# Column halves for scores and weight grams, transposes in transpose mode, and a new order of the first steps, in an attention and feed-forward kernel on one core

## The chip, the cores and the metric

The program runs on one core of a Trainium2 chip. The time is device time in microseconds (us) of one execution, and the number given for a kernel is a median over runs: for the kernel before 741.81 us, of three runs from 740.6 to 742.11. TensorE, VectorE, ScalarE, GpSimd and SyncE are called PE, DVE, ACT, POOL and SP, as the profile does; PEld is the load of the stationary operand of a matmul.

## The reference

The inputs are float32: q, k, v (4 batches, 8 heads, 768 positions, 64 per head), 8 memory keys and values, and the weights of two mixing layers. Each chunk of 32 queries sees 8 memory keys and 56 neighbours, 64 keys in all.

```python
for c in range(768 // 32):
    l, r = max(0, 32 * c - 16), min(768, 32 * c + 32 + 8)
    scores = scale * q[:, :, 32 * c:32 * c + 32] @ concat(mem_k, k[:, :, l:r]).T
    a = softmax(scores)
    out[:, :, 32 * c:32 * c + 32] = a @ concat(mem_v, v[:, :, l:r])
x = out with its heads side by side                      # 4 x 768 x 512
gate = sigmoid(causal convolution of x over 5 steps, per channel)
x = (gate * (x @ w_val)) @ w_out                         # 512 x 512 each
xn = (x - mean) / sqrt(var + 1e-6) * g_ln
out = x + relu(xn @ w_ch1) @ w_ch2                       # 512 x 2048, 2048 x 512
```

The four weight matrices and the convolution come as words of 8 bytes, which the kernel turns into float32 itself.

## The kernel before

The 3072 positions are cut into 24 sub-blocks of 128 (`SUB`), which are grouped into 13 blocks: the first of one sub-block, eleven of two, the last of one. Each block goes through three streams. Attention (`a`): scores into PSUM (`s_ps`), maximum, difference and Exp into `sc`, `normalize`, a transpose to `pT`, and the product with v (`pv`), which ACT and DVE copy to `xT`. Mixing (`x`, in `mix`): the gate `gt` as a chain of five taps on ACT and DVE, `val` = x times `Wv`, the output product `yps`, its statistics and the normalised `xn`. Feed-forward (`f`): `ch1` writes `c_ps`, ACT and DVE make `h` of it, and `ch2` adds into `acc`.

Matmuls come in two kinds. The first sub-blocks use float32 operands: the attention of the first five (`attention32`, as `NA32` counts three blocks), the mixing of the first two blocks, the feed-forward of block 0. All others use a pair of float16 tiles, a high and a low part, in three passes (`PASSES`), so that a score of one head pair and group takes three matmuls. A score matmul has both chunks of a group as its 128 output rows (`bd`, block-diagonal, 2 chunks x 2 heads x 32 queries) and all 96 keys of the group as columns. Of these each chunk uses 64: four copies on ACT (L251) pick them out of two PSUM tiles, and DVE takes the maximum (L254) and the difference (L255) from `sc` in SBUF.

Before the float16 kind can start, each weight needs one power of two as its scale, which is found from the sum of its squares. A weight arrives in pieces of 1 MB (20 in all); each is converted by ACT (`top`, L162) and DVE (L163), and PE then sums its squares as the diagonal of a gram matrix: eight matmuls of 128 x 128 per piece (L198, tile `gram`). `weight_scale` multiplies with `eye` and reduces (L205, L206). Then `split_weight` makes the two parts (ACT L218, DVE L219). Four float32 transposes of 128 x 128 make `pT` (L331) in the first five sub-blocks, and `xnT` (L538) in the first two blocks; they are matmuls with `eye`. Later transposes go by DMA.

The order of work is written out by hand. `PLAN` is a string of steps: `w` starts the fetch of a weight piece, `l` the loads of a sub-block, `m`, `1` and `2` take a step of the mixing weights, of the first and of the second feed-forward weight, and `a`, `x`, `f` a step of the three streams. After `PLAN` the string `STEADY` is walked through once for each block. A scheduler then puts the instructions of each engine in a fixed order, and each engine runs its own list strictly in that order. `fill` issues idle matmuls at the start (`FILLS`). `ps` is a pool of four PSUM tiles for scores, transposes, `pv`, `val` and `yps`.

Of the kernel before, what the change touches and what calls it, by code (L numbers as in the profile page):

```python
# [8 lines left out]
F32 = mybir.dt.float32  # L9
# [24 lines left out]
NA32 = 3  # L34
# [5 lines left out]
PLAN = "w1 m1 a5 m1 l1 w3 x1 w2 m1 x5 a1 l1 a2 m1 w1 x1 w1 x2 a2 m1 1_1 a1 1_1 w1 a1 w2 1_1 x1 1_1 a2 1_1 a1 1_1 x1 w1 1_1 x1 1_1 x1 2_1 l1 w1 1_1 f1 x1 w1 x4 m1 2_1 x1 w2 f1 1_1 2_1 m1 f1 2_2 x1 f1 1_2 a1 2_1 a1 x1 a1 f1 2_2 m1 w1 l1 f1 a1 1_2 f1 2_1 a1 2_1 a2 2_1 x1 1_1 m1 w1 a1 2_1 a2 1_2 2_2 f1 x1 2_3"  # L40
# [14 lines left out]
def chunk_attention_moe_kernel(ctx: ExitStack, tc: tile.TileContext,  # L55
# [34 lines left out]
    eye = const.tile([P, P], F32, name="eye")  # L90
    g_one = const.tile([P, 1], F32, name="g_one")
# [97 lines left out]
    def gram(W, j):  # L189
        if j == 0:  # L190
            tag = "acc0" if W in (Wv, W1) else "acc1"
            W.acc = ps_a.tile([P, 512], F32, tag=tag, name="gram")
            W.gram = W.acc[:, 0:P]

        w = W.src(j).bitcast(BF16).rearrange("p (n w) -> p n w", w=2)
        for c in range(8):
            x = w[:, c * P:(c + 1) * P, 1]
            nc.tensor.matmul(out=W.gram, lhsT=x, rhs=x, start=(j == 0 and c == 0), stop=(j == W.n - 1 and c == 7))  # L198

    def weight_scale(W, bits, name, factor=None):  # L200
# [4 lines left out]
        nc.vector.tensor_tensor(out=diag, in0=W.gram, in1=eye, op=ALU.mult)  # L205
# [21 lines left out]
    first16 = sum(sizes[:NA32])  # L227
# [15 lines left out]

    def exponentials(i, s_ps, c_exp):
# [50 lines left out]
    def attention32(n, d, u):  # L295
# [11 lines left out]
        for e in range(2):  # L307
# [52 lines left out]
    def attention(n, d, u):  # L360
# [45 lines left out]
        s_ps = []  # L406
        for g in range(2):
            t = ps.tile([P, HP, KEYS], F32, tag="ps", name="s_ps")
            for hp in range(HP):
                for x, (r0, r1) in enumerate(PASSES):  # L410
                    nc.tensor.matmul(out=t[:, hp, :],  # L411
                                     lhsT=bd[r0][:, hp, g].rearrange("p c e q -> p (c e q)"),
                                     rhs=k2[r1][:, hp, g, :], start=(x == 0), stop=(x == 2))
            s_ps.append(t)
# [39 lines left out]
    def open_block(j):  # L454
        d = blk[j] = {"T": blocks[j][1] * SUB, "iv": {}, "split": j > 0, "f32": j < NF32, "a32": j < NA32}
# [3 lines left out]
        return d  # L459

    def mix(j):
# [5 lines left out]
        for hp in range(HP):  # L467
# [11 lines left out]
        nc.scalar.activation(out=gt[:, :, 0:T], in_=gt[:, :, 0:T], func=AF.Tanh, scale=0.5)  # L479
# [6 lines left out]
        for w in range(2):  # L486
# [17 lines left out]
        xn = d["xn"] = [xn_p.tile([P, KC, 2 * SUB], F16, tag=f"xn{r}", name=f"xn{r}") for r in range(2)] if d["split"] else \  # L504
            [b_p.tile([P, KC, 2 * SUB], F16, tag="hg0", name="xnf").rearrange("p k t -> p (k t)").bitcast(F32).rearrange("p (k t) -> p k t", t=SUB)]
        mv = sm_p.tile([P, 2, 2], F32, tag="mv", name="mv")
        for u in range(n):
# [12 lines left out]
            if u == n - 1:  # L520
# [10 lines left out]
        for u in range(n):  # L531
# [3 lines left out]
            if j < NPET:  # L535
                t = ps.tile([P, KC, P], F32, tag="ps", name="xnT")
                for kc in range(KC):
                    nc.tensor.matmul(out=t[:, kc, :], lhsT=xh[:, kc * P:(kc + 1) * P], rhs=eye, start=True, stop=True)  # L538
                if d["split"]:
# [5 lines left out]
                nc.vector.tensor_tensor(out=xn[0], in0=t, in1=g_sb.rearrange("p (k o) -> p k o", o=1).to_broadcast([P, KC, P]),  # L545
                                        op=ALU.mult)
# [13 lines left out]
    def ch1(d, w):  # L560
# [70 lines left out]
    if True:  # L631
# [17 lines left out]
        pieces = [(W, jj) for W in (Wv, Wo, W1, W2) for jj in range(W.n)]  # L649
        fetched = [0]  # L650
# [91 lines left out]
        to_f32(cw_raw, cw_sb.rearrange("p k c -> p (k c)"))  # L742
        count = dict.fromkeys(streams, 0)
# [3 lines left out]
        per = {"a": lambda j, n: (5 if j < NA32 else 8) * n, "x": lambda j, n: 8 + 2 * n, "f": lambda j, n: NM * n * SUB // 256}  # L747
# [61 lines left out]
```

## Time and profile before

| | |
|---|---|
| median of 3 runs | 741.81 us (740.6 to 742.11) |
| the profiled execution: its time | 740.43 us |
| its span | 738.6 us |
| chain that ended last, share of PE | 85% |
| the same, share of DVE, ACT | 8%, 5% |
| DMA, mean over the span | 91 GB/s |

The profiled execution took 740.43 us, of which the span, from the first to the last recorded instruction, is 738.6 us. The chain that ended last is followed back from the last instruction to whatever released it; an engine with a high share of it is the one whose work set the end. Busy time alone says less: matmuls are pipelined, so that the start of one row and the start of the next give a better duration than the row's own length, which has the pipeline's drain in it.

### The profile page before, as it was taken

What the parts mean: (1) busy time and instruction counts of PE and PEld (TensorE: products, weight loads), DVE (VectorE), ACT (ScalarE), POOL (GpSimd) and SP (SyncE); (2) the same over time, 40 slices, a digit from 0 to 9 for tenths busy, and PEclk for the clock granted to TensorE, in tenths of its full rate; (3) what the DMA queues carried; (4) which work ended last, traced back from release to release, by engine and by line L of the source; (5) the groups of instructions that cost most, each with busy time, mean ns of one, the idle gap of its engine ahead of it and who ended that gap; (6) DMA issues with size and microseconds to landing.
All of it is one profiled execution on the core that took longest, in us unless ns stands there. A gap on an engine that the chain in (4) does not pass through costs nothing.

```text
span 738.6 us, 15525 instructions
## 1 busy us (share of the span) xinstructions
PE 724.9 (98%) x6461; PEld 512.1 (69%) x6461; DVE 509.2 (69%) x1124; ACT 392.5 (53%) x684; POOL 10.6 (1%) x35
## 2 busy tenths in 40 slices
PE   8889999999999999999999999999999999999998
PEld 7777676667767757757757767767767766767676
DVE  4979989768658768768668668668667668651321
ACT  5867967647537537537546546546555554420210
POOL 2000010000000000000000000000000000000000
PEclk9999999999999999999999999999999999999999
DMA  9992623142132133132142153043043011010010
GB/s 357 417 401 109 228 65 89 37 113 72 52 79 86 37 86 94 34 89 95 29 95 94 19 104 94 16 100 101 16 101 100 16 30 43 16 29 30 1 43 15
DMA packets 62262, 67.08 MB, mean 91 GB/s; under 512 B 45680, under 2 KB 45936, under 8 KB 62192
## 3 DMA queue, kind: packets, MB, share of 16 engines
q1 hardware_dynamic: 61904, 66.07, 29.5%
q8 instruction: 50, 0.82, 0.5%
q14 instruction: 20, 0.16, 0.1%
q10 hardware_dynamic: 288, 0.02, 0.0%
HBM read 49.30 MB, written 6.29 MB: 75 GB/s over the span
## 4 chain that ended last, share of the span: by engine, by line
PE 85%; DVE 8%; ACT 5%; issue 1%; DMA 0%; ACTq 0%; DVEq 0%
PE acc L598 32%; PE c_ps L570 32%; PE yps L511 8%; PE val L493 7%; PE s_ps L411 2%; PE pv L441 2%; DVE gt L475 2%; DVE w L163 1%; ACT top L162 1%; PE pv L345 1%; ACT w L218 1%; ACT sc L251 1%; DVE w L219 1%; ACT xT L289 1%; DMA g_sb<-in_g_ln_dram 0%
## 5 line engine op out<-in xcount | busy, mean ns | idle before, releaser
L598 PE MATMUL acc<-w,h 128*128 128x512 f16 (+3 forms) x1184 | 267.0, 377 | 0.1
L570 PE MATMUL c_ps<-xn,w 128*128 128x256 f16 (+1 forms) x2304 | 254.8, 268 | 0.0
L570 PEld LDWEIGHTS <-w 128*128 128x128 f16 x2304 | 215.4, 98 | 36.9 <-issue 0.6
L598 PEld LDWEIGHTS <-h 128*128 128x128 f16 x1152 | 109.5, 98 | 114.1 <-DVE h L575 1.8
L575 DVE SCALAR_TENSOR_TENSOR h<-c_ps,h 128x512 f16<-128x512 f32 x92 | 62.9, 683 | 54.0 <-ACT h L573 53.9
L573 ACT ACTIVATE h<-c_ps 128x512 f16<-128x512 f32 (+1 forms) x96 | 56.5, 588 | 79.1 <-PE c_ps L570 77.5
L475 DVE SCALAR_TENSOR_TENSOR gt<-xT,cw_sb,gt 128x256 f32<-128x256 f32 (+1 forms) x208 | 83.4, 458 | 1.6 <-ACT gt L471 1.5
L511 PE MATMUL yps<-wo,hg 128*128 128x512 f16 x252 | 58.3, 379 | 0.2
L493 PE MATMUL val<-x,wv 128*128 128x256 f16 (+1 forms) x528 | 56.9, 268 | 0.0
L493 PEld LDWEIGHTS <-wv 128*128 128x128 f16 x528 | 49.7, 98 | 5.5
L251 ACT ACTIVATE sc<-s_ps 64x256 f32<-64x256 f32 x96 | 36.2, 377 | 25.4 <-PE s_ps L411 22.5
L511 PEld LDWEIGHTS <-hg 128*128 128x128 f16 x252 | 23.2, 98 | 26.7 <-DVE hg L499 0.6
L377 ACT ACTIVATE vs<-vt 128x1024 bf16<-128x1024 f32 x19 | 19.9, 1048 | 39.8 <-PE pv L441 39.8
L498 ACT ACTIVATE hg<-gt 128x512 f16<-128x512 f32 (+1 forms) x22 | 13.4, 610 | 47.2 <-DVE gt L495 47.2
L550 ACT ACTIVATE xh<-xh 128x512 f16<-128x512 f32 x21 | 13.2, 630 | 44.8 <-DMA xn<-xh 23.8
L605 DVE SCALAR_TENSOR_TENSOR y<-acc,co_w,y 128x512 f32<-128x512 f32 (+2 forms) x24 | 16.5, 725 | 28.9 <-PE acc L598 28.8
L551 DVE TENSOR_TENSOR xh<-xh,xh 128x512 f16<-128x512 f32 x21 | 14.5, 692 | 27.4 <-DMA xn<-xh 19.5
L291 DVE TENSOR_SCALAR xT<-pv,c_pv 64x256 f32<-64x256 f32 x38 | 17.0, 488 | 19.3 <-ACT xT L289 19.2
L422 ACT ACTIVATE p<-sc 128x512 f16<-128x512 f32 x19 | 12.0, 630 | 33.0 <-DVE sc L270 32.9
L393 DVE SCALAR_TENSOR_TENSOR bd<-qt,s,bd 64x512 f16<-64x512 f32 x38 | 28.3, 744 | 0.7
L495 DVE SCALAR_TENSOR_TENSOR gt<-gt,val 128x512 f32<-128x512 f32 (+1 forms) x26 | 16.6, 646 | 15.7 <-PE val L493 15.7
L392 ACT ACTIVATE bd<-qt,s 64x512 f16<-64x512 f32 x38 | 27.1, 712 | 0.5
(136 smaller groups left out, 809.8 us busy)
## 6 DMA issues: line engine op xcount, KB each, us to landing
vt<-in_v_dram SPq DMA_DIRECT2D x24, 512.0 KB, 3.9
kt<-in_k_dram SPq DMA_DIRECT2D x24, 384.0 KB, 3.6
qt<-in_q_dram SPq DMA_DIRECT2D x24, 256.0 KB, 2.7
out_dram<-y SPq DMA_DIRECT2D x23, 256.0 KB, 2.1
w<-in_w_ch_dram SPq DMA_DIRECT2D x5, 1023.5 KB, 9.3
raw<-in_w_ch_dram SPq DMA_DIRECT2D x4, 1023.8 KB, 13.5
w<-in_w_ch_dram SPq DMA_DIRECT2D x4, 1023.8 KB, 14.2
raw<-in_w_ch_dram SPq DMA_DIRECT2D x3, 1023.5 KB, 5.3
```

Source lines behind the costliest of these rows:

```text
L251: nc.scalar.activation(out=by_group[pp, :, g, :], in_=s_ps[g][pp, :, ch * CHUNK:ch * CHUNK + NSEEN], func=AF.Copy)
L291: nc.vector.tensor_scalar(out=o, in0=t[pp, :, :, e, :], scalar1=c_pv if isinstance(c_pv, float) else c_pv[pp], scalar2=None, op0=ALU.mult)
L377: nc.scalar.activation(out=v2[0].bitcast(BF16), in_=vt, func=AF.Square, accum_out=ss[:, 2:3])
L392: nc.scalar.activation(out=hi, in_=src, func=AF.Copy, scale=s[pp, 0:1])
L393: nc.vector.scalar_tensor_tensor(out=lo, in0=src, scalar=s[pp, 0:1], in1=hi, op0=ALU.mult, op1=ALU.subtract)
L475: nc.vector.scalar_tensor_tensor(out=o, in0=xT[:, hp, 0:n, kk:kk + SUB], scalar=cw_sb[:, kk, hp:hp + 1], in1=o, op0=ALU.mult, op1=ALU.add)
L493: nc.tensor.matmul(out=t[:, u, 0:T], lhsT=l, rhs=r, start=(x == 0), stop=(x == len(todo) - 1))
L511: nc.tensor.matmul(out=t, lhsT=l, rhs=r, start=(x == 0), stop=(x == len(todo) - 1))
L570: nc.tensor.matmul(out=t[:, u * T:(u + 1) * T], lhsT=l, rhs=r, start=(x == 0), stop=(x == len(todo) - 1))
L573: nc.scalar.activation(out=h[0], in_=t, func=AF.Relu)
L575: nc.vector.scalar_tensor_tensor(out=h[1], in0=t, scalar=0.0, in1=h[0], op0=ALU.max, op1=ALU.subtract)
L598: nc.tensor.matmul(out=a[:, 0:n], lhsT=l, rhs=r, start=(m == 0 and x == 0), stop=(m == NM - 1 and x == len(todo) - 1))
```

## The change

Scores: `scores` writes one PSUM tile of 8 x 64 columns. The two chunks of a group become two matmuls, each with 64 columns of `bd` as its stationary operand and its own 64 keys as the moving one; chunk 0 writes output partitions 0 to 63, chunk 1 partitions 64 to 127. The matmuls of a sub-block go from 24 of 128 x 96 to 48 of 64 x 64 in float16, and from 8 to 16 in float32 (each of these runs as two instructions). The four copies on ACT go; maximum and difference read PSUM.

Grams: a piece takes sixteen matmuls of 64 x 64, even column groups into partitions 0 to 63, odd into 64 to 127, and the diagonal is picked with `eye2`, two 64-wide unit matrices, which POOL makes. Transposes by PE (`flip`) use the transpose mode in place of a matmul with `eye`. The float32 `xn` of block 0 lies in two tiles of its own and is written by two instructions of half the width. `PLAN` is new, and its end now holds the steps of a block which `STEADY` held before. The branches of `QD`, `DIAG`, `POWR`, `ORDER` and `TP` are not taken; `A32` is the old `NA32`.

```diff
-NA32 = 3
+A32 = 3
+NFF = 1
+COLS = 1
+POWR = 0
+PET = 1
+GC = 1
+QD = 0
+DIAG = 0
...
-PLAN = "w1 m1 a5 m1 l1 w3 x1 w2 m1 x5 a1 l1 a2 m1 w1 x1 w1 x2 a2 m1 1_1 a1 1_1 w1 a1 w2 1_1 x1
+PLAN = "w1 a4 l1 a1 w3 m2 w1 m1 a1 x1 w1 1_1 m1 l1 x1 w1 x1 w1 x2 w1 x3 a2 w1 x1 1_1 a1 m1 a2 w1 a1
...
         w = W.src(j).bitcast(BF16).rearrange("p (n w) -> p n w", w=2)
+        if GC:
+            for c in range(16):
+                x = w[:, c * 64:(c + 1) * 64, 1]
+                o = c % 2 * 64
+                nc.tensor.matmul(out=W.gram[o:o + 64, 0:64], lhsT=x, rhs=x, start=(j == 0 and c < 2), stop=(j == W.n - 1 and c > 13))
+            return
...
+            diag = diag[:, 0:64]
+            nc.vector.tensor_tensor(out=diag, in0=W.gram[:, 0:64], in1=eye2, op=ALU.mult)
...
+    def scores(b2, k2):
+        todo = passes(range(len(b2)), range(len(b2)))
+        if COLS:
+            t = ps.tile(WIDE, F32, tag="ps", name="s_ps")
+            for hp in range(HP):
+                for g in range(2):
+                    for x, (r0, r1) in enumerate(todo):
+                        for ch in range(2):
+                            nc.tensor.matmul(out=t[ch * 64:(ch + 1) * 64, 2 * hp + g, :],
+                                             lhsT=b2[r0][:, hp, g, ch].rearrange("p e q -> p (e q)"),
+                                             rhs=k2[r1][:, hp, g, ch * CHUNK:ch * CHUNK + NSEEN],
+                                             start=(x == 0), stop=(x == len(todo) - 1))
+            return [t]
...
-        for g in range(2):
-            for ch in range(2):
-                pp = slice(ch * 64, (ch + 1) * 64)
-                nc.scalar.activation(out=by_group[pp, :, g, :],
-                                     in_=s_ps[g][pp, :, ch * CHUNK:ch * CHUNK + NSEEN], func=AF.Copy)
+        src = sc
+        if COLS:
+            src = s_ps[0]
...
-        nc.vector.tensor_reduce(out=mx, in_=sc, axis=AX.X, op=ALU.max)
-        nc.vector.tensor_tensor(out=sc, in0=sc, in1=mx.to_broadcast(WIDE), op=ALU.subtract)
+        nc.vector.tensor_reduce(out=mx, in_=src, axis=AX.X, op=ALU.max)
+        nc.vector.tensor_tensor(out=sc, in0=src, in1=mx.to_broadcast(WIDE), op=ALU.subtract)
...
+    def flip(o, x):
+        if PET:
+            nc.tensor.transpose(out=o, in_=x, identity=eye)
+        else:
+            nc.tensor.matmul(out=o, lhsT=x, rhs=eye, start=True, stop=True)
...
-            nc.tensor.matmul(out=t[:, hp, :], lhsT=sc[:, 2 * hp:2 * hp + 2, :].rearrange("p g k -> p (g k)"), rhs=eye,
-                             start=True, stop=True)
+            flip(t[:, hp, :], sc[:, 2 * hp:2 * hp + 2, :].rearrange("p g k -> p (g k)"))
...
+        if GC:
+            nc.gpsimd.tensor_tensor(out=eye2, in0=eye[:, 0:64], in1=eye[:, 64:128], op=ALU.add)
```

How the lists of the engines moved is shown at two places of DVE's list. The first is the first softmax of the kernel before; `wv` with `top` is the conversion of the first piece of that weight, whose ACT half (`top`) runs beside it:

```order
L254 TENSOR_REDUCE mx<-sc 128x8
L255 TENSOR_TENSOR sc<-sc,mx 128x512
L163 SCALAR_TENSOR_TENSOR wv<-w_113,top_115 128x1024
L259 MEMSET sc 64x4x16
L267 TENSOR_REDUCE sum<-sc 128x8
L268 TENSOR_SCALAR sum<-sum 128x8
L269 RECIPROCAL rs<-sum 128x8
L270 TENSOR_TENSOR sc<-sc,rs 128x512
```

DVE at the same place in the changed kernel, whose line numbers are its own (L304 maximum, L305 difference, L175 conversion):

```order
L304 TENSOR_REDUCE mx<-s_ps 128x8
L305 TENSOR_TENSOR sc<-s_ps,mx 128x512
L309 MEMSET sc 64x4x16
L317 TENSOR_REDUCE sum<-sc 128x8
L318 TENSOR_SCALAR sum<-sum 128x8
L175 SCALAR_TENSOR_TENSOR wv<-w_114,top_116 128x1024
L319 RECIPROCAL rs<-sum 128x8
L320 TENSOR_TENSOR sc<-sc,rs 128x512
```

The conversion has moved from ahead of the sum to behind it, ahead of the reciprocal; on ACT its `top` has moved from ahead of the Exp to behind it. The second place is DVE's list around the gate of the first block in the kernel before; the `gt<-xT` rows are the taps, the `mx` is that of the next sub-block:

```order
L475 SCALAR_TENSOR_TENSOR gt<-xT,cw_sb,gt 128x128 x13
L163 SCALAR_TENSOR_TENSOR wo<-w_113,top_115 128x1024
L475 SCALAR_TENSOR_TENSOR gt<-xT,cw_sb,gt 128x128 x2
L254 TENSOR_REDUCE mx<-sc 128x8
L475 SCALAR_TENSOR_TENSOR gt<-xT,cw_sb,gt 128x128
L255 TENSOR_TENSOR sc<-sc,mx 128x512
L163 SCALAR_TENSOR_TENSOR wo<-w_113,top_114 128x1024
L495 SCALAR_TENSOR_TENSOR gt<-gt,val 128x2x128 x2
```

DVE at the same place in the changed kernel (L561 is a tap, L582 the product with `val`):

```order
L561 SCALAR_TENSOR_TENSOR gt<-xT,cw_sb,gt 128x128 x15
L175 SCALAR_TENSOR_TENSOR wo<-w_114,top_116 128x1024
L561 SCALAR_TENSOR_TENSOR gt<-xT,cw_sb,gt 128x128
L304 TENSOR_REDUCE mx<-s_ps 128x8
L225 TENSOR_TENSOR diag<-gram,eye_102 128x64
L582 SCALAR_TENSOR_TENSOR gt<-gt,val 128x2x128 x2
L305 TENSOR_TENSOR sc<-s_ps,mx 128x512
L175 SCALAR_TENSOR_TENSOR wo<-w_114,top_116 128x1024
```

The product with `val` has moved ahead of the difference and of the second `wo` conversion, and 15 of the 16 taps, 13 before, stand ahead of the first one. SP's list, the loads and the weight pieces, stands as it did through all of this part.

## Rows read from the trace of the kernel before

**Rows 1.** The page's first part: busy us, share of the span, instructions.

```profile
PE 724.9 (98%) x6461; PEld 512.1 (69%) x6461; DVE 509.2 (69%) x1124; ACT 392.5 (53%) x684; POOL 10.6 (1%) x35
```

**Rows 2.** Busy us by stretch (from:to); clock, DMA share and GB/s last.

```profile
0.00:50.00 50.00, 40.66 (x451) 36.72 (x452) 34.85 (x85) 31.13 (x49) 4.97 (x13) 1.00 0.98 392
50.00:124.00 74.00, 72.87 (x533) 53.63 (x532) 70.20 (x131) 60.09 (x87) 2.50 (x5) 1.00 0.41 145
124.00:700.00 576.00, 575.75 (x5105) 394.85 (x5104) 395.75 (x896) 297.10 (x542) 3.17 (x17) 1.00 0.24 62
```

**Rows 3.** PE's waits: us in total, times, longest.

```profile
PE gram L198 <- DVE w L163: 2.4, 2, 2.2
PE gram L198 <- DVE wo L163: 2.2, 1, 2.2
PE s_ps L411 <- DVE ks L396: 0.5, 1, 0.5
```

**Rows 4.** Groups of PE and ACT by form: busy us, mean ns; idle before.

```profile
L411 PE MATMUL s_ps<-ks,bd 128*128 128x96 f16 x456 | 22.7, 206 | 0.5 <-DVE ks L396 0.5
...
L251 ACT ACTIVATE sc<-s_ps 64x256 f32<-64x256 f32 x96 | 36.2, 377 | 25.4 <-PE s_ps L411 22.5 <-PE s_ps L320 1.7
...
L162 ACT ACTIVATE top<-w 128x1024 f16<-128x1024 bf16 x13 | 17.5, 1356 | 1.7 <-DMA w<-in_w_val_dram 1.5
```

**Rows 5.** PE's timeline in the steady stretch: start us, us, instructions.

```profile
147.37 1.18 PE L411 MATMUL s_ps<-ks,bd 128*128 128x96 f16 x24
148.39 2.75 PE L598 MATMUL acc<-w,h 128*128 128x512 f16 x12
150.98 2.78 PE L570 MATMUL c_ps<-xn,w 128*128 128x256 f16 x24
...
158.81 5.34 PE L598 MATMUL acc<-w,h 128*128 128x512 f16 x24
164.09 0.87 PE L441 MATMUL pv<-pT,vs 64*128 64x64 f16 x48
164.89 2.79 PE L570 MATMUL c_ps<-xn,w 128*128 128x256 f16 x24
```

**Rows 6.** PE's timeline at the start: float32 forms, grams, the first float16 `c_ps`.

```profile
12.40 1.13 PE L331 MATMUL pT_ps<-eye,sc 128*128 128x128 f32 x8 [0.24 <-DVE sc L270]
...
32.81 2.00 PE L345 MATMUL pv<-pT,vt 64*128 64x64 f32 x32 [0.56 <-DVE pT L335]
34.74 2.03 PE L320 MATMUL s_ps<-kt,bd 128*128 128x96 f32 x16
36.60 0.62 PE L198 MATMUL gram<-w 128*128 128x128 bf16 x8
...
43.16 0.64 PE L198 MATMUL gram<-w 128*128 128x128 bf16 x8 [2.21 <-DVE w L163]
43.63 0.44 PE L570 MATMUL c_ps<-xnf,w 128*128 128x128 f32 x2
43.90 1.08 PE L331 MATMUL pT_ps<-eye,sc 128*128 128x128 f32 x8
44.81 1.28 PE L570 MATMUL c_ps<-xnf,w 128*128 128x128 f32 x10
...
103.48 5.08 PE L570 MATMUL c_ps<-xn,w 128*128 128x256 f16 x45
```

**Rows 7.** DVE's timeline at the first scores, and where it fills up.

```profile
7.67 0.69 DVE L254 TENSOR_REDUCE mx<-sc 128x8 f32<-128x512 f32 x1 [2.40 <-ACT sc L251]
8.39 0.69 DVE L255 TENSOR_TENSOR sc<-sc,mx 128x512 f32<-128x512 f32 x1
9.07 1.23 DVE L163 SCALAR_TENSOR_TENSOR wv<-w,top 128x1024 int32<-128x1024 int32 x1
...
49.20 0.77 DVE L291 TENSOR_SCALAR xT<-pv 64x256 f32<-64x256 f32 x2 [2.36 <-ACT xT L289]
50.61 1.01 DVE L475 SCALAR_TENSOR_TENSOR gt<-xT,cw_sb,gt 128x256 f32<-128x256 f32 x2 [0.64 <-ACT gt L471]
```

More of the change, by code (lines that the diff above doesn't have):

```diff
@@ L242, in load @@
                 nc.sync.dma_start(out=st["v"], in_=v[b, i])
+    def scores(b2, k2):
[11 more added lines that the diff above has]
+            return [t]
+        s_ps = []
+        for g in range(2):
+            t = ps.tile([P, HP, KEYS], F32, tag="ps", name="s_ps")
+            for hp in range(HP):
+                for x, (r0, r1) in enumerate(todo):
+                    nc.tensor.matmul(out=t[:, hp, :],
+                                     lhsT=b2[r0][:, hp, g].rearrange("p c e q -> p (c e q)"),
+                                     rhs=k2[r1][:, hp, g, :], start=(x == 0), stop=(x == len(todo) - 1))
+            s_ps.append(t)
+        return s_ps
     def exponentials(i, s_ps, c_exp):
@@ L306, in attention32 @@
             d["iv"][u] = inv
-        for e in range(2):
+        for e in range(0 if QD else 2):
             pp = slice(e * 64, (e + 1) * 64)
@@ L315, in attention32 @@
         yield
-        s_ps = []
-        for g in range(2):
-            t = ps.tile([P, HP, KEYS], F32, tag="ps", name="s_ps")
+        if QD:
+            t = ps.tile(WIDE, F32, tag="ps", name="s_ps")
             for hp in range(HP):
-                nc.tensor.matmul(out=t[:, hp, :], lhsT=bd32[:, hp, g].rearrange("p c e q -> p (c e q)"),
-                                 rhs=kt[:, hp, g, :], start=True, stop=True)
-            s_ps.append(t)
+                for g in range(2):
+                    for ch in range(2):
+                        for e in range(2):
+                            o, pp, c = ch * 64 + e * CHUNK, slice(e * 64, (e + 1) * 64), 2 * g + ch
+                            nc.tensor.matmul(out=t[o:o + CHUNK, 2 * hp + g, :], lhsT=qt[pp, hp, c * CHUNK:(c + 1) * CHUNK],
+                                             rhs=kt[pp, hp, g, ch * CHUNK:ch * CHUNK + NSEEN], start=True, stop=True,
+                                             tile_position=(e * 64, o) if TP else None)
+            s_ps = [t]
+        else:
+            s_ps = scores([bd32], [kt])
         if n == 0:
@@ L405, in attention @@
         yield
[L406 to L414, printed above, removed]
+        s_ps = scores(bd, k2)
         yield
@@ L459, in open_block, with diagonals @@
         return d
+    def flip(o, x):
+        if PET:
+            nc.tensor.transpose(out=o, in_=x, identity=eye)
+        else:
+            nc.tensor.matmul(out=o, lhsT=x, rhs=eye, start=True, stop=True)
+    diags = {}
+    def diagonals(part):
+        if not diags:
+            homes = [(x_p, "x0"), (x_p, "x0"), (x_p, "x1"), (x_p, "x1"), (b_p, "hg1")]
+            for kk, (p, tag) in zip(range(KW - 1, -1, -1), homes):
+                t = p.tile([P, HP, 2 * SUB], F16, tag=tag, name="dg")
+                t = t.rearrange("p a b -> p (a b)").bitcast(F32).rearrange("p (a t) -> p a t", t=P)
+                for hp in range(HP):
+                    diags[kk, hp] = t[:, hp, :]
+        for n, (kk, hp) in enumerate(diags):
+            if n % 2 == part:
+                if DG_ENG == "v":
+                    nc.vector.tensor_scalar(out=diags[kk, hp], in0=eye, scalar1=cw_sb[:, kk, hp:hp + 1], scalar2=None, op0=ALU.mult)
+                elif DG_ENG == "g":
+                    nc.gpsimd.tensor_scalar(out=diags[kk, hp], in0=eye, scalar1=cw_sb[:, kk, hp:hp + 1], scalar2=None, op0=ALU.mult)
+                else:
+                    nc.scalar.activation(out=diags[kk, hp], in_=eye, func=AF.Copy, scale=cw_sb[:, kk, hp:hp + 1])
     def mix(j):
@@ L466, in mix @@
         gt = b_p.tile([P, HP, 2 * SUB], F32, tag="gt", name="gt")
-        for hp in range(HP):
+        if j < DIAG:
+            if not diags:
+                diagonals(0)
+                diagonals(1)
+            yield
+            for w in range(2):
+                t = ps.tile([P, 2, 256], F32, tag="ps", name="gps")
+                for u in range(2):
+                    for kk in range(KW):
+                        nc.tensor.matmul(out=t[:, u, 0:T], lhsT=diags[kk, 2 * w + u], rhs=xT[:, 2 * w + u, 0:n, kk:kk + SUB],
+                                         start=(kk == 0), stop=(kk == KW - 1))
+                nc.scalar.activation(out=gt[:, 2 * w:2 * w + 2, 0:T], in_=t[:, :, 0:T], func=AF.Tanh, scale=0.5)
+                yield
+            yield
+        for hp in range(HP if j >= DIAG else 0):
             o = gt[:, hp, 0:T].rearrange("p (u t) -> p u t", t=SUB)
@@ L537, in mix @@
                 for kc in range(KC):
-                    nc.tensor.matmul(out=t[:, kc, :], lhsT=xh[:, kc * P:(kc + 1) * P], rhs=eye, start=True, stop=True)
+                    flip(t[:, kc, :], xh[:, kc * P:(kc + 1) * P])
                 if d["split"]:
@@ L544, in mix @@
                     continue
[L545 to L546 removed]
+                g3 = g_sb.rearrange("p (k o) -> p k o", o=1)
+                for r in range(2):
+                    nc.vector.tensor_tensor(out=f32[r][:, :, u * SUB:(u + 1) * SUB], in0=t[:, 2 * r:2 * r + 2, :],
+                                            in1=g3[:, 2 * r:2 * r + 2, :].to_broadcast([P, 2, P]), op=ALU.mult)
                 yield
@@ L649, in chunk_attention_moe_kernel @@
         pieces = [(W, jj) for W in (Wv, Wo, W1, W2) for jj in range(W.n)]
+        if ORDER:
+            left = {c: iter([(W, jj) for jj in range(W.n)]) for c, W in zip("vo12", (Wv, Wo, W1, W2))}
+            pieces = [next(left[c]) for c in ORDER]
         fetched = [0]
@@ L742, in chunk_attention_moe_kernel @@
         to_f32(cw_raw, cw_sb.rearrange("p k c -> p (k c)"))
+        if DIAG:
+            diagonals(0)
+            diagonals(1)
         count = dict.fromkeys(streams, 0)
```

44 lines of the change are left out of this document (32 added, 12 removed).

## The prediction

> **What bounds the kernel now.** I read the page's totals first, then busy time by stretch, PE's waits, and last the timelines. PE is busy 98% of the span, DVE and ACT 69% and 53% [rows 1]. From 124 to 700 us PE is busy 575.75 of 576.00 us [rows 2], and its waits there are nothing: whatever PE no longer does in this stretch shortens the kernel by just that, and whatever ACT or DVE no longer do is worth nothing. So the 1.5 us of ACT copies in each sub-block (96 of 377 ns [rows 4]) are worth nothing from there on.
>
> The first 124 us are another matter. Up to 50 us PE is busy 40.66 us, some of that idle matmuls, with the DMA engines at 0.98 [rows 2]; what PE waits for is DVE: conversions of weight pieces, 2.2 us at a time [rows 3]. From 50 to 124 PE is busy 72.87 of 74 us and DVE 70.20 [rows 2]. DVE is as good as full there, so that PE work taken away before 124 us only comes back as PE waiting, unless DVE gets its list done sooner too. [...]
>
> **The change part by part.** *Float16 scores, 19 sub-blocks* (456 matmuls before, 24 each [rows 4]). Before: from 147.37 to 148.39, 1.02 us, 42 ns a matmul [rows 5]. After: 48 matmuls of half the rows and 64 columns. The trace has no matmul in column halves. The nearest row is `pv`: 48 float16 matmuls with 64 columns whose two row halves alternate, 164.09 to 164.89, 0.80 us or 17 ns each [rows 5]. Entering that mode costs something too: the 24 `acc` matmuls ahead of it take 158.81 to 164.09, 5.28 us, where twice the 12 from 148.39 to 150.98 make 5.18 [rows 5], so 0.10. If column halves run like row halves, a sub-block takes 0.90, 0.12 less; I take 0.11. That is the best end; 64 columns in full, unshared, would be far slower.
>
> The worse end comes from the float32 rows. A float32 score matmul, 96 columns, takes two instructions of 116 ns (16 in 34.74 to 36.60), and a transpose of 128 columns 114 ns (8 in 43.90 to 44.81) [rows 6]. Fewer columns don't make it quicker, so the load of its 128 stationary columns sets the pace, some 116 ns; in `pv`, whose row halves alternate, it is 60 ns each (32 in 32.81 to 34.74) [rows 6]: two loads lie side by side. In float16 a load of 128 columns is hidden under a matmul of 42 ns [rows 5], so it is a quicker kind of load. If 64-column loads lose that and go at the float32 pace, they take 58 ns, 29 ns with two side by side: 48 x 29 + 0.10 = 1.49 us, 0.47 more for each sub-block. Not side by side it is 48 x 58 + 0.10 = 2.88, 1.86 more. I take the `pv` rate, as the row nearest in type, count and shape, and keep the other as a rival.
>
> [...]
>
> *Float32 scores, 5 sub-blocks.* 1.86 us before [rows 6]. After, 32 instructions with 64-column loads: 29 ns each if the halves share, 0.93 + 0.10, so 0.83 less; not shared, 32 x 58 = 1.86, nothing less. I take 0.83, 4.2 in all, of PE time.
>
> *Transposes by PE*, 8 groups of four (five `pT`, three `xnT`): 0.91 us a group [rows 6]. The trace has no transpose mode. Between 0.23 (four at the 59 ns of a bfloat16 gram matmul, 8 in 43.16 to 43.63 [rows 6]) and 0.91 as now, I take 0.46, one instruction with one load in place of two: 8 x 0.45 = 3.6 of PE time.
>
> *Grams*, 20 pieces: 0.47 us [rows 6]. After, sixteen at 17 ns and 0.10 to enter the mode: 0.37, so 2.0 less in all; at 29 ns 0.56, 1.9 more in all.
>
> These last three, 9.8 us of PE time, all lie before 124 us, where DVE's list decides. So I follow DVE. Its own work hardly changes: maximum and difference are 0.69 us each [rows 7] and read PSUM instead, four rows for the gram diagonals get half as wide, `xn` of block 0 becomes two half rows. I reckon 0.9 us less up to the second `xnT` of block 1, from counting rows in both lists, mostly because one row that made the low part of x now stands behind it.
>
> What counts is then DVE's waiting. (1) First softmax: the maximum waits 2.40 us for ACT's copies [rows 7]. Without them and with shorter scores it starts some 1.6 us sooner. But the `wv` conversion (1.23 us [rows 7]) lay under the Exp; now it stands ahead of the reciprocal, and its ACT half (1.36 [rows 4]) comes behind the Exp. What is late next is that conversion, and it takes back about 1.1. `pT` starts near 11.9 instead of 12.40 [rows 6], its transposes give 0.45 more, and `pv` and all behind it come 1.0 us sooner. On PE 86 idle matmuls now stand between the scores and the grams (before 62, and 24 further on); at 59 ns each, that of a gram matmul, they end at 5.9 + 5.1 = 11.0, just ahead of `pT`, so they cost nothing unless the scores end a microsecond later than I think. (2) First gate: a conversion, a difference and a maximum lay in its path, now a conversion and a maximum; the product with `val` no longer waits for the 0.69, and the second `wo` conversion follows it. I take another 0.8: `yps` still waits for that conversion with its second half. (3) From there to 50.61 [rows 7] DVE is mostly full of conversions. The 2.36 us wait for `pv` at 46.84 [rows 7] moves ahead of a conversion whose data is there, but that conversion's ACT half then waits for the copies of `pv`; I carry on 1.9 sooner, no more.
>
> With 0.9 less work and a little less waiting, the first float16 `c_ps` starts 3.0 us sooner than 103.48 [rows 6]. Behind it the new order asks for `ks` and the low half of the second `h` about 1.2 and 0.7 us before DVE has them; before, PE waited 0.5 for `ks` [rows 3]. Set against shorter PE rows in between, the first 124 us give 2.8. For the range: from 1.5 lost (the moved conversion and the earlier asked `h` cost more than I see) to 9.8 gained (DVE keeps up).
>
> Sum: 18 float16 sub-blocks that lie where PE is full x 0.11 = 2.0, and 2.8 at the start: 4.8 us off the profiled execution's 740.43 (span 738.6 and 1.8 around it), 735.6. The median of the runs is 1.4 above that execution, so 737.0. A measurement of this kernel can tell about 0.2%, 1.5 us.
>
> **The rivals.** *Slow loads of 64 columns.* Every score sub-block in the PE-bound stretch takes 1.49 instead of 1.02: 18 x 0.47 = 8.5 lost, the start gives 2.8 still, since DVE bounds it: 740.43 + 5.7 = 746.1, median 747.5. The whole comes out slower once a score instruction takes over 22 ns (48 x 22.4 + 0.10 - 1.02 = 0.156, times 18 the 2.8 of the start). For it: all loads in the trace that are seen to set a pace are slow ones. Against it: `pv` with 17 ns for as narrow a matmul. [...] With loads not side by side it would be 740.43 - 2.8 + 18 x 1.86 = 771; I give this 0.03 of the 0.24 below.
>
> *PE bounds the start after all.* All PE time that goes counts: 9.8 + 19 x 0.11 = 11.9, so 728.5, median 729.9. For it: PE is at 72.87 of 74 us in 50 to 124. Against it: DVE with 70.20 beside it [rows 2].
>
> *Nothing.* Column halves cost what full matmuls did (21 ns an instruction), and the order of the start gives back at one place what it takes at another, as in (1): 740.4, median 741.8.
>
> **How the numbers follow.** Forecast 0.50 (median 737.0, its own range 733 to 741), slow loads 0.24, PE-bound start 0.12, nothing 0.14. The range has to take in the slow loads side by side and the PE-bound start: 729 to 748; serial loads stay out. Faster by over 0.2%: nine tenths of the forecast, the PE-bound case and a little of "nothing", 0.59. Slower: nearly all of the slow loads and a little of the others, 0.26. Within 0.2%: 0.15.
>
> **What would show it.** In the steady stretch, score rows of 48 matmuls that start 0.9 us ahead of the next row show the forecast; 1.4 to 1.5 us, with PE still at 576 of 576, the slow loads. At the start: `pT` near 11.9 and its four transposes in under 0.5; DVE still at 95% in 50 to 124 us with PE's busy time down by several us and more waits for DVE; the first float16 `c_ps` near 100.5. If PE stays as full as now before 124 us and `c_ps` comes near 95, the PE-bound rival was right. A wait of over 2 us for the second `h` would show that the new order costs more than I reckon. The prediction is wrong if float16 scores take over 1.1 us or the first float16 `c_ps` starts after 103.

## The result and the profile after

The changed kernel takes 746.07 us, median of 4 runs (743.79 to 746.86), beside 741.38 us (4 runs, 740.6 to 742.11) for the kernel before: a ratio of 1.0054, 95% interval 1.0033 to 1.0075. It is slower by half a per cent, where 737.0, a gain of 0.65%, was forecast. The profiled execution took 743.79 us, with a span of 741.8; it is the quickest of the four.

The page's first part answers to [rows 1]: PE has as much to do as before within 1.6 us, ACT 38 us less.

```profile
PE 723.3 (98%) x7125; PEld 503.5 (68%) x7125; DVE 507.2 (68%) x1125; ACT 354.3 (48%) x588; POOL 12.6 (2%) x36
```

Busy time of the changed kernel by stretch (columns as in [rows 2]):

```profile
0.00:50.00 50.00, 37.15 (x464) 32.04 (x466) 31.05 (x82) 24.36 (x34) 6.93 (x14) 0.83 0.93 356
50.00:124.00 74.00, 73.28 (x739) 52.96 (x740) 69.86 (x131) 56.77 (x76) 2.45 (x5) 1.00 0.48 170
124.00:700.00 576.00, 574.10 (x5526) 389.48 (x5525) 395.34 (x888) 268.28 (x471) 3.19 (x17) 1.00 0.24 62
```

Two things are new in the first row. The granted clock, the last column but two, is 0.83 where it was 1.00, and DVE did 3.8 us less by then. In the third row PE is busy 574.10 us of 576 where it was 575.75. PE's waits say what for (us in total, times, longest):

```profile
PE pT_ps L510 <- POOL eye L733: 3.4, 1, 3.4
PE pT_ps L510 <- DVE sc L320: 2.3, 2, 2.0
PE s_ps L274 <- ACT bd L362: 1.9, 1, 1.9
PE acc L694 <- DVE h L671: 1.3, 4, 0.6
```

The first is a wait for POOL, which no row of before has. POOL's timeline of the changed kernel (start, us, instruction, idle time before it):

```profile
4.26 0.20 POOL L732 MEMSET eye<- 128x128 f32 x1
14.10 0.38 POOL L742 PARTITION_ALL_REDUCE g_max<-g_one  x1 [9.63 <-issue]
14.36 0.35 POOL L733 TENSOR_SCALAR_AFFINE_SELECT eye<-eye 128x128 f32<-128x128 f32 x1
...
25.93 1.90 POOL L736 TENSOR_TENSOR eye<-eye 128x64 f32<-128x64 f32 x1 [11.14 <-issue]
```

and the same stretch of the kernel before:

```profile
4.61 0.35 POOL L644 PARTITION_ALL_REDUCE g_max<-g_one  x1
4.85 0.35 POOL L637 TENSOR_SCALAR_AFFINE_SELECT eye<-eye 128x128 f32<-128x128 f32 x1
```

Before, the reduction follows at once and the unit matrix `eye` is there at 5.2. Now POOL stands 9.63 us ahead of the reduction and 11.14 us ahead of the addition that makes `eye2`, in which it waited for nothing that the profile shows, and `eye` comes at 14.7. The first transposes need it:

```profile
10.98 0.35 PE L212 MATMUL gram<-wv 128*64 128x64 bf16 x10
14.77 1.12 PE L510 MATMUL pT_ps<-eye,sc 128*128 128x128 f32 x4 [3.44 <-POOL eye L733]
16.67 3.68 PE L400 MATMUL pv<-pT,vt 64*128 64x64 f32 x32 [0.48 <-DVE pT L390]
...
105.66 3.66 PE L666 MATMUL c_ps<-xn,w 128*128 128x256 f16 x32
...
147.30 2.78 PE L666 MATMUL c_ps<-xn,w 128*128 128x256 f16 x24
150.01 0.95 PE L274 MATMUL s_ps<-ks,bd 128*64 128x64 f16 x48
150.89 2.76 PE L694 MATMUL acc<-w,h 128*128 128x512 f16 x12
```

The `pv` behind them takes 3.68 us, where it took 2.00 [rows 6]. Behind that wait the granted clock is down, 0.50 in the two microseconds from 18 on, which lie within this `pv`:

```profile
10.00:20.00 10.00, 6.08 (x71) 5.40 (x68) 3.92 (x6) 1.81 (x2) 0.69 (x3) 0.71 1.04 410
18.00:20.00 2.00, 2.00 (x23) 2.00 (x22) 0.33 (x1) 0.00 (x0) 0.00 (x0) 0.50 1.07 434
20.00:30.00 10.00, 8.88 (x100) 8.40 (x98) 5.79 (x18) 5.93 (x11) 2.11 (x2) 0.61 1.01 410
```

The first float16 `c_ps` starts at 105.66, 2.2 us later than before [rows 6] and past the 103 that the prediction named as the sign of being wrong.

### The profile page after: what moved, and what is told of

It is laid out like the page before. It is cut to its first block, busy times and chain, and to the rows that moved or that the text cites. A ratio compares the mean times of both kernels' runs of the same rounds, so it can differ in the third digit from the quotient of the medians.

```text
span 741.8 us, 16731 instructions
## 1 busy us (share of the span) xinstructions
PE 723.3 (98%) x7125; PEld 503.5 (68%) x7125; DVE 507.2 (68%) x1125; ACT 354.3 (48%) x588; POOL 12.6 (2%) x36
## 4 chain that ended last, share of the span: by engine, by line
PE 81%; DVE 10%; ACT 4%; DMA 2%; issue 2%; POOL 0%; SPq 0%; DVEq 0%
PE c_ps L666 31%; PE acc L694 29%; PE val L580 9%; PE yps L602 6%; PE s_ps L274 2%; PE pv L488 2%; DMA xn<-xh 2%; PE pv L400 1%; DVE h L671 1%; PE gram L212 1%; ACT xT L339 1%; DVE bs L609 1%; DVE sc L320 1%; DVE xh L647 1%; DVE sc L305 1%
## 5 line engine op out<-in xcount | busy, mean ns | idle before, releaser
L561 DVE SCALAR_TENSOR_TENSOR gt<-xT,cw_sb,gt 128x256 f32<-128x256 f32 (+1 forms) x208 | 83.1, 455 | 4.2 <-ACT gt L557 4.1
L582 DVE SCALAR_TENSOR_TENSOR gt<-gt,val 128x512 f32<-128x512 f32 (+1 forms) x26 | 16.7, 645 | 16.1 <-PE val L580 16.0
L317 DVE TENSOR_REDUCE sum<-sc 128x8 f32<-128x512 f32 x24 | 16.4, 685 | 13.1 <-ACT sc L306 12.8
```

The lines of the kernel that those rows point to most:

```text
L561: nc.vector.scalar_tensor_tensor(out=o, in0=xT[:, hp, 0:n, kk:kk + SUB], scalar=cw_sb[:, kk, hp:hp + 1], in1=o, op0=ALU.mult, op1=ALU.add)
```

## The experiments

A is the theory that POOL's late unit matrix makes the loss. Its rivals are that PE's work at the start has become too thin and the clock falls, and that DVE's and ACT's instructions stand in a worse order. Their letters shift in the texts of what was expected: the clock is C in e1 to e4, D in e5 to e8, B in e9 to e12 and C again from e13 on; the order is B in e1 to e4 and D from e13 on. E, in e5 to e8, says that the clock costs nothing. Ratios are to the kernel before, run beside; its medians were 741.7 to 743.5.

**e1, e2: the addition.** e1 makes `eye2` on DVE; e2 is the kernel before with the addition on POOL, its result unused.

```diff
-            nc.gpsimd.tensor_tensor(out=eye2, in0=eye[:, 0:64], in1=eye[:, 64:128], op=ALU.add)
+            nc.vector.tensor_tensor(out=eye2, in0=eye[:, 0:64], in1=eye[:, 64:128], op=ALU.add)
```

> The changed kernel, with the one addition that makes eye2 moved from POOL to DVE. Theory A (POOL: that addition puts a second load of POOL code into the program, the unit matrix comes at 14.7 us instead of 5.2, PE waits 3.4 us for it and then runs at half clock): the unit matrix is there near 5, the first transposes start at 11.7 to 12.0, the granted clock is 1.00 from 10 to 30 us, the first float16 c_ps comes at 99 to 101, and the time is 735.5 to 738.5. Theory B (the new order itself costs, by PE's waits for bd and sc between 40 and 49 us): the first transposes come sooner but the first float16 c_ps not before 103, time 740.5 to 744. Theory C (transposes in transpose mode let the clock fall): half clock still from about 14 to 28 us, time 743 to 746.

> The kernel before, with nothing added but the POOL addition that makes eye2, whose result nobody reads. Theory A: the unit matrix comes near 14.5 us, the first transposes wait 2 to 2.5 us for it (they started at 12.40), and the time is 743 to 748. Theories B and C: POOL's addition is off the path, 741 to 742.

e2: 747.27 us, ratio 1.0076 (1.0059 to 1.0092), 5.6 us for an instruction whose result nobody reads. The lists of PE, DVE, ACT and SP are those of before, row for row. Its first transposes wait 2.05 us for `eye` and start at 15.44 (before 12.40), and its first float16 `c_ps` starts at 109.17, 5.7 us later than before. Its POOL timeline:

```profile
14.76 0.38 POOL L646 PARTITION_ALL_REDUCE g_max<-g_one  x1 [10.30 <-issue]
15.03 0.35 POOL L638 TENSOR_SCALAR_AFFINE_SELECT eye<-eye 128x128 f32<-128x128 f32 x1
27.49 0.51 POOL L640 TENSOR_TENSOR eye<-eye 128x64 f32<-128x64 f32 x1 [12.04 <-issue]
```

So A holds for the addition's cost, and the addition delays what stands ahead of it too. What POOL does in these 10 us the profile doesn't show. The list of its instructions has one more row (`ISA`) ahead of the addition, as the reduction has one. In the program these rows are named `PseudoReloadLibraryIndex`, with index 1 ahead of the reduction and index 0 ahead of the addition; the kernel before, e1 and e17 have only the first, and POOL has no such gap in them. That it is the second row that brings the gaps, of 9.6 to 12.0 us, is an estimate from this; no run shows what fills them. All six runs of e2, at 746.46 to 748.48, lie above all those of before beside them (744.06 at most), so the price was paid in each.

e1: 744.71 us, ratio 1.0033 (1.0015 to 1.005). The reduction is back at 4.61, but A's 735.5 to 738.5 is missed: the kernel is still slower than before. That looked like a second cause, and the clock was the suspect: in e1's twelve runs the time goes from 740.78 to 746.87 as the mean clock goes from 0.995 to 0.984.

**e3 to e8: one part out at a time.** All but e3 and e7 start from e1; e4 has the old `PLAN`, e8 adds 68 idle matmuls that read `sc` or `pT`.

```diff
-COLS = 1
-PET = 1
-GC = 1
+COLS = 0   # e3, e5
+PET = 0    # e3, e6
+GC = 0     # e3, e7 (no eye2)
-PLAN = "w1 a4 l1 a1 w3 m2
+PLAN = "w1 m1 a5 m1 l1 w3   # e4
+        if n in HOLD3:      # e8: 16 behind the first pv, 40 behind the second
+            hold(HOLD3[n], pT[:, 0, :])
```

> The changed kernel with its new order alone: scores, transposes and grams as in the kernel before, no eye2. Theory A: the order is not at fault, 738.5 to 741.5 and no late unit matrix. Theory B: slower than before by 1 to 4 us, 742.5 to 745.5, with waits for bd and sc between 38 and 50 us. Theory C: as A.

> All of the change but the order (the old one), with eye2 made on DVE. Theory A: 736 to 739.5, within 1.5 of the first kernel of this set. Theory B: 735 to 738.5 and at least 2 us faster than that kernel. Theory C: half clock behind the first transposes and no faster than 741.

> The kernel with eye2 on DVE (744.7 us, granted clock 0.984 to 0.995 over the span), with the scores as in the kernel before. Theory D (what the changed kernel still loses lies in the clock: its shorter PE rows leave PE idle more at the start, and the granted clock falls to half there; each fall costs 2 to 4 us): the mean clock is higher than with column halves, 0.993 to 1.0, and the time 741 to 743.5. Theory E (the clock costs nothing, since DVE bounds the start; column halves bring a gain of 1 to 2 us after 124 us): slower, 745 to 747.

> The kernel with eye2 on DVE, with the transposes as plain matmuls again. Theory D1 (a transpose in transpose mode does not count as work for the clock): mean clock 0.995 or more, time 740.5 to 743. Theory D2 (only PE's waits count, whatever it did before): mean clock as with transpose mode, 0.984 to 0.995, 744 to 745.5. Theory E: 744.5 to 746, by 0.45 us for each group that PE waits for.

> The changed kernel with the grams as they were, 128 by 128 and eight of them, so without eye2 and without the POOL addition. Theory D: mean clock a little above that with the small grams, 0.987 to 0.997, 742 to 744.5. Theory E: the 0.1 us a piece are hidden under DVE, 744 to 745.

> The kernel with eye2 on DVE, with 68 idle matmuls more in the places where PE waits in the first 40 us: 16 behind the first pv, 12 behind the second transposes, 40 behind the second pv. Theory D: the granted clock stays at 1.00 up to 40 us, the mean is 0.997 or more, and the time 738 to 740.5. Theory E: the clock stays up, but the time is 743.5 to 746, since PE had time to spare.

| | us | ratio (95%) |
|---|---|---|
| e3 new order alone | 744.08 | 1.0032 (1.0016, 1.0047) |
| e4 old order, all parts | 744.0 | 1.002 (1.0002, 1.0037) |
| e5 without column-half scores | 744.27 | 1.0031 (1.0006, 1.0056) |
| e6 without transpose mode | 739.46 | 0.9947 (0.9928, 0.9967) |
| e7 without small grams | 738.76 | 0.9935 (0.9913, 0.9958) |
| e8 with idle matmuls | 738.75 | 0.9946 (0.9925, 0.9967) |

Against e1, taking out either thinning, or adding idle work, gives 0.9 to 1%: it reads like proof of the clock theory. The forecasts fit less well: e8's time fell into D's range, but its clock (0.988 to 0.998) did not; e6 and e7 came out below all of theirs and e5 between its two. Of the earlier runs e3 is in the range of B, the order, and e4 in that of C.

**e9 to e12: parts alone, and the best.** e9 and e10 have one part each with the old `PLAN` (and block 0's `xn` in two halves, as the changed code writes it); e10's `eye2` is DVE's. e11 is e7 with 40 idle matmuls where it waited 2.48 us for `bd`.

```diff
+COLS = 0; PET = 1; GC = 0   # e9, old PLAN
+COLS = 0; PET = 0; GC = 1   # e10, old PLAN
+GC = 0; HOLD3 = {1: 40}     # e11
+COLS = 1; PET = 0; GC = 0   # e12
```

> One part alone on the kernel before: only the float32 transposes in transpose mode; scores, grams, unit matrix and the order as before. Theory B (both transposes and grams made thinner are needed before the clock falls in most executions): clock stays at or above 0.995, the transposes save a little PE time at the start that DVE mostly gives back: 738 to 742 us. Rival (the transpose mode by itself lets the clock fall): half clock for some microseconds between 12 and 45, mean clock 0.985 to 0.992, 743 to 746 us.

> One part alone on the kernel before: only the grams 64 by 64 in column halves (with the folded unit matrix made by VectorE, so that GpSimd does as before); scores, transposes and the order as before. Theory B: clock at or above 0.995, 739 to 742 us. Rival (the thinner grams by themselves let the clock fall): half clock in the start, mean 0.985 to 0.992, 743 to 746 us.

> Changed kernel without the column-half grams and their unit matrix, and with 40 idle matmuls behind the second block's pv, where the first float32 scores of the third sub-block waited 2.48 us for ACT and the clock then fell for some 6 us. Theory B: that fall goes and nothing else moves: mean clock 0.997 or more, about 2 to 3 us less than without the idle matmuls, 736 to 737 us. Rival (the time lost to that fall is DVE's anyway, as DVE bounds the start): no change, 738.5 to 739 us, with more PE waits.

> Changed kernel with only the column-half scores and the new order: grams and transposes as before, no folded unit matrix. Theory B (with both fat the clock holds, and the sooner scores and the order pay): clock at or above 0.995, 738 to 740 us. Rival (the transposes and grams do pay too once the clock holds): slower than the kernel without one of them, 740.5 to 742 us.

| | us | ratio (95%) |
|---|---|---|
| e9 transpose mode alone | 749.92 | 1.009 (1.0071, 1.011) |
| e10 small grams alone | 742.09 | 0.9983 (0.997, 0.9996) |
| e11 e7 with idle matmuls | 739.77 | 0.9948 (0.9926, 0.997) |
| e12 column-half scores and new order | 736.98 | 0.9917 (0.9897, 0.9936) |

e9 broke the theory: the slowest kernel of all, with a mean clock of 0.995, and a wait of 2.7 us for `bd` where before waits 0.3. The lists tell why. With the same `PLAN`, the scheduler of e9 had put ACT's `bd` behind a weight conversion and the copies of `pv`. It places by its own estimate of times, so writing transposes in another way moves instructions of other engines. Set against the list of before, e9's has 42 rows of difference on ACT and 91 on DVE; e6's against e1's 16 and 60, e8's against e1's 40 and 96. Runs e1 and e3 to e10 and e12 therefore each changed two things. Of the others, e10 came out 0.1 us above the range of B, and e12 1.0 us below it. Only e2 and e11 changed one thing, and e11, whose lists but for PE's are those of e7, gained nothing by its idle matmuls (0.9948 beside 0.9935): the fall of the clock moved from the stretch 35 to 41 us (0.50 in e7 from 36 to 40) to that of 42 to 52 (0.50 in e11).

**e13 to e16: the same order, another amount of PE work.** Each is built twice: the first build gives the order of every engine's list, and the second, with the other kind of work, is held to it.

```diff
+            for e in order:
+                for p, n in zip(order[e], order[e][1:]):
+                    tc.add_manual_dep(traced[e][n], traced[e][p].name, after, reason="order")
```

> The order of every engine of the changed kernel with its folded unit matrix on VectorE (ratio 1.0033 to before), word for word, but the float32 transposes as plain matmuls with the unit matrix. Theory C (the clock: TensorE's thin work at the start is what lets it fall): clock at or above 0.994, ratio 0.993 to 0.997. Theory D (the order of VectorE and ScalarE): ratio 1.002 to 1.005 still.

> The order of every engine of the kernel with only the column-half scores and the new order (ratio 0.9917 to before), word for word, but the float32 transposes in transpose mode. Theory C: the clock falls once for some microseconds, ratio 0.993 to 0.998. Theory D: the clock stays at 1.00 and the ratio at 0.990 to 0.992, as eight transposes of 0.9 us become 0.45 us at a start that VectorE bounds.

> The kernel before, in the order of every engine word for word, but the float32 transposes in transpose mode. Theory C: the clock falls in the start, for instance where the first sub-blocks' pT stand before or behind the waits of 2.2 us near 24 and 42 us; ratio 1.002 to 1.008. Theory D (the 1.009 of the transposes alone came from the order that the scheduler made of it): clock at 1.00, ratio 0.997 to 1.000.

> The order of every engine of the changed kernel with its folded unit matrix on VectorE (ratio 1.0033 to before), word for word, with 68 idle matmuls added behind the first and second sub-blocks' pv and between the second's transposes. Theory C: clock at or above 0.994, ratio 0.993 to 0.998. Theory D: ratio 1.002 to 1.006 still.

| | us | ratio (95%) | free order |
|---|---|---|---|
| e13 e1, transposes as matmuls | 744.74 | 1.0033 (1.0021, 1.0046) | e6 0.9947 |
| e14 e12, transposes in transpose mode | 736.2 | 0.9923 (0.9896, 0.995) | e7 0.9935 |
| e15 before, transposes in transpose mode | 744.08 | 1.0024 (1.0005, 1.0043) | e9 1.009 |
| e16 e1, idle matmuls | 743.3 | 1.0015 (0.9997, 1.0032) | e8 0.9946 |

e13 against e6 is the test: the same work, 0.9% apart, and e13 stands where e1 stood (1.0033). So between e1 and e6 it is the order that counts, D, and not the transposes. By which path the order costs is open in part: with it go the waits and the falls of the clock (mean 0.991 to 0.993 in e13, 0.993 to 0.997 in e6). One wait is to be seen in e1's PE timeline at the first float16 `c_ps`, which starts at 102.08 in e6:

```profile
105.37 0.38 PE L666 MATMUL c_ps<-xn,w 128*128 128x256 f16 x2
107.55 3.43 PE L666 MATMUL c_ps<-xn,w 128*128 128x256 f16 x30 [1.80 <-DVE xn L636]
```

and on DVE in e1:

```profile
103.75 0.69 DVE L304 TENSOR_REDUCE mx<-s_ps 128x8 f32<-128x512 f32 x1
104.36 1.28 DVE L241 SCALAR_TENSOR_TENSOR w<-w,w_s 128x1024 f16<-128x1024 f32 x1
105.55 0.75 DVE L410 SCALAR_TENSOR_TENSOR x<-xT,s,x 128x512 f16<-128x512 f32 x1
106.22 0.68 DVE L305 TENSOR_TENSOR sc<-s_ps,mx 128x512 f32<-128x512 f32 x1
106.81 0.68 DVE L636 TENSOR_TENSOR xn<-xnT,xn 128x512 f16<-128x512 f32 x1
```

In the changed kernel's DVE list `xn` follows the maximum directly:

```profile
103.19 0.69 DVE L304 TENSOR_REDUCE mx<-s_ps 128x8 f32<-128x512 f32 x1
103.80 0.68 DVE L636 TENSOR_TENSOR xn<-xnT,xn 128x512 f16<-128x512 f32 x1
```

In e1 a weight product, `x` and the difference stand between. e13 and e16, in the same order, wait 1.3 and 1.8 us for this `xn`. e1's own loss thus comes from e1's order, which is not that of the changed kernel.

e14 shows what the thinner transposes do to the clock when nothing else moves. From 30 to 40 us, e12 and then e14:

```profile
30.00:40.00 10.00, 8.11 (x113) 7.24 (x111) 9.50 (x30) 7.33 (x11) 0.44 (x1) 1.00 1.02 421
```

```profile
30.00:40.00 10.00, 8.75 (x92) 7.73 (x91) 8.64 (x27) 6.29 (x10) 0.20 (x1) 0.66 1.02 419
```

The clock falls, as C had it, and yet the first float16 `c_ps` starts at 99.37, in e12 at 100.00, and the ratio moves by 0.0006, within its interval; it lies between the ranges of C and D. With the order held the clock is 0.66 beside 1.00 in this stretch, but around e14's other transposes it stays at 1.00, as it does through four of e15's ten runs, and e14's time shows no price. e15 is 0.24% slower than before, in C's range. That this is the clock's price isn't shown: the four runs at 1.00 take 742.06 to 743.74, where the six of before at 1.00 beside them take 740.47 to 742.08. Its profiled execution, at 747.72 the slowest of the ten, does not settle it: the grams on PE wait 1.5 us there for DVE's `sc`, as in no row of before, the clock falls twice (0.59 and 0.56 from 28 to 32 us, 0.50 from 46 to 48), and `acc` waits 2.8 us for `h`, 0.1 us in before. e16's 0.2% against e1 lies within the two intervals, just under D's range.

**e17, e18: the changed kernel itself.** e17 makes `eye2` on POOL by masks, with the lists of PE, DVE, ACT and SP held to the changed kernel's. e18 does too, but holds DVE, ACT and SP to e12's order.

```diff
-            nc.gpsimd.tensor_tensor(out=eye2, in0=eye[:, 0:64], in1=eye[:, 64:128], op=ALU.add)
+            nc.gpsimd.memset(eye2, 0.0)
+            for base in (0, -64):
+                nc.gpsimd.affine_select(out=eye2, in_=eye2, pattern=[[-1, 64]], base=base, channel_multiplier=1,
+                                        compare_op=ALU.not_equal, fill=1.0)
```

> The changed kernel, the order of VectorE, ScalarE, SyncE and TensorE word for word; only the folded unit matrix is made on GpSimd by a memset and two masks instead of an addition. Theory A (the addition's delay of the unit matrix): the all-reduce starts near 4.6 again, the wait of 3.4 us ahead of the first transposes goes, ratio 0.993 to 1.001, 3 to 6 us less than the changed kernel. Rival (the order of VectorE and ScalarE costs as much as in e1): ratio 1.002 to 1.005.

> All parts of the change (column halves, transpose mode, small grams, the folded unit matrix by masks on GpSimd) with the order of VectorE, ScalarE and SyncE taken word for word from the kernel with only the column-half scores and the new order (ratio 0.9917 to before). Theory D (the order decides, thin TensorE work does little): ratio 0.989 to 0.994. Theory C (thin TensorE work lets the clock fall and that decides): mean clock under 0.993 and ratio 0.998 to 1.004.

e17: 741.56 us, ratio 0.9966 (0.9947 to 0.9984), as A had it; 0.9% less than the changed kernel, with no row of the other engines' lists moved. POOL and the first transposes of e17:

```profile
4.70 0.35 POOL L753 PARTITION_ALL_REDUCE g_max<-g_one  x1
4.93 0.35 POOL L738 TENSOR_SCALAR_AFFINE_SELECT eye<-eye 128x128 f32<-128x128 f32 x1
5.18 0.30 POOL L744 TENSOR_SCALAR_AFFINE_SELECT eye<-eye 128x64 f32<-128x64 f32 x1
```

```profile
11.88 0.63 PE L515 MATMUL pT_ps<-eye,sc 128*128 128x128 f32 x4 [0.43 <-DVE sc L325]
```

The transposes wait 0.43 us for DVE, as in before (0.24 [rows 6]). The clock still falls (0.77, 0.88, 0.80 and 0.67 in the four stretches of 10 us from 10 on), and its runs follow it: 737.63 us at a mean of 0.995, 743.58 at 0.986. How much of that is the clock's price, and how much only goes with it, no run here separates.

e18: 739.04 us, ratio 0.9944 (0.9931 to 0.9958), just above D's range. All parts of the change together win once the unit matrix is on time. That e12's order is better for them than the changed kernel's isn't clear of the two intervals. The best medians are still e12's (0.9917) and e14's (0.9923), without the small grams.

## Why the prediction was wrong

*What it left out.* No term of the sum was for POOL. The change part listed what the grams save and did not price the addition that makes `eye2`, neither its own time nor what stands behind it on its queue. That is the step that failed: it costs 0.8 to 0.9% (e2, e17 against the changed kernel), 5.6 to 6.5 us, more than the whole forecast gain of 4.8. Without it the change is faster, 0.9966, where 737.0 of 741.81 is 0.9935, outside e17's interval: about half of the forecast gain is there, and the terms below were off as well. One sign was there: the new instruction stood in the diff.

*No term for the clock.* The granted clock of 1.00 in all three stretches [rows 2] was true of one execution. Of the 110 executions of the kernel before that ran beside the experiments, 38 have a mean of 1.00 and the others 0.995 to 0.999; the changed kernel's four have 0.986 to 0.989. A mean of 1.00 in the profile says that the clock did not fall in that execution, not that it won't after a wait such as the 3.4 us here.

*Float16 scores, 2.0 us*: 150.01 to 150.89 is 0.88, and the `c_ps` ahead of them lasts 2.71 (147.30 to 150.01) where the next lasts 2.62 (153.49 to 156.11). That makes 0.97 against 1.02 [rows 5]: 0.05 saved, not 0.11, some 0.9 us in 18 sub-blocks: the term was over twice too large, as a matmul takes 18 ns and not 17. And even this did not come out of the whole. From the `yps` at 144.71 to the one at 696.59 are 551.88 us, in before 142.16 to 693.48, 551.32. In between, `acc` waits for DVE's `h` at three places, in before at none (the fourth wait of the list above stands ahead of them, at 125.35):

```profile
273.21 3.19 PE L694 MATMUL acc<-w,h 128*128 128x512 f16 x14
276.59 2.33 PE L694 MATMUL acc<-w,h 128*128 128x512 f16 x10 [0.19 <-DVE h L671]
...
444.79 2.33 PE L694 MATMUL acc<-w,h 128*128 128x512 f16 x10 [0.19 <-DVE h L671]
...
613.35 2.33 PE L694 MATMUL acc<-w,h 128*128 128x512 f16 x10 [0.55 <-DVE h L671]
```

That is 0.93 us of idle time, and 0.17 more at each place, since the 14 `acc` ahead of it take 3.19 where 3.02 is their pace: 1.44 in all. Without it 550.44 would be left, the 0.9 less. So PE time saved there does shorten the kernel, as the prediction had it; what it missed are the waits. The saving alone doesn't make them: e8, e11 and e16 have the same scores, no such wait and 550.44 to 550.51 us, while e9 and e15, with the scores of before, wait some 3 us for `h` there. What decides whether DVE is late for `h` stays open. The rival of slow 64-column loads is refuted: 48 in 0.88 is 18 ns each.

*Float32 scores, transposes and grams* were sized right. Where the granted clock is 1.00, the scores of the changed kernel take 0.98 to 1.09 us where 1.03 was forecast, four transposes 0.43 at 35.20 and 0.44 at 94.09 where 0.46 was, a gram piece 0.37 at 56.51 as forecast. That little of what PE saves there shortens the start was right too: in e14 the eight groups of transposes are 3.2 us shorter in all than in e12, the first float16 `c_ps` comes 0.6 us sooner, and the time is e12's. How much of the rest DVE took back and how much the lower clock isn't separated. The sign named for it, PE's busy time down by several us in 50 to 124 us, did not come: 73.28 in the changed kernel, 72.87 before. The rival of a start bounded by PE asked for a `c_ps` near 95; no run comes there, 98.69 in e18 being the soonest.

*The start, 2.8 us.* In the profiled execution DVE had `sc` ready at 11.6, so `pT` would have begun near the forecast 11.9; in e17 it does, at 11.88. Further on the size isn't shown. By the medians, e17's gain of 2.5 us (0.34% of 743.36) and its 0.5 lost in the steady stretch (551.84) leave 3.0 for the start, where 2.8 was forecast. By the traces there is nothing: e17's first float16 `c_ps` starts at 103.61, 0.1 later than before [rows 6], and not 3.0 sooner. But the two traces were not taken side by side, and beside e17 the fastest execution of before took 742.41, 2.0 more than the profiled one. In e12, e14 and e18, in another order, `c_ps` starts 3.5 to 4.8 us sooner than before. The order was the weak point: the same parts gave from 0.9944 to 1.0033 as the scheduler laid them.

*The loss in the profiled execution* adds up: 2.55 by the `yps` mark (144.71 against 142.16) and 0.56 from there to the next make 3.1 of the 3.2 us between the spans; the other three runs, at 745.86 to 746.86, lost 2 to 3 more.

## What to carry to other kernels

Price every instruction that a change adds, also on an engine that is busy 1% of the time: look at what is queued around it there and at who waits for that. When a scheduler lays out the lists, a run with one part taken out is a run with another order; hold the lists before you call a difference a cause. A clock of 1.00 in one profile is no promise for the changed kernel, nor for the next execution of the same one.

## What the hardware showed that was not expected

With a small addition on POOL, in this program with a partition reduction, POOL stood 9.6 to 10.3 us ahead of the reduction and 11.1 to 12.0 ahead of the addition (changed kernel, e2); with a memset and masks in its place, 0.15 to 0.30 us each, it stood at neither (e17). Reading scores from PSUM did not slow DVE: the maximum takes 0.69 us in the changed kernel, as from SBUF before [rows 7]. The half-width column matmuls in float16 took 18 ns each (48 in 0.88 us), nearly what `pv`'s row halves took (17 [rows 5]).
